# A planner that writes every engine's order: its timing constants, engine occupancy, GpSimd/VectorE exclusion and DMA landings replaced

## The chip, the cores and the metric

The kernel runs on one core of a Trainium2 chip. The metric is device time in microseconds for one launch. The core has five engines with a queue each: TensorE (PE, with its weight loads PEld), VectorE (DVE), ScalarE (ACT), GpSimd (POOL) and SyncE (SP, which here only issues DMAs). Each queue runs its instructions in the order in which the program wrote them, and waits on semaphores for the others.

## The reference

One transformer block on 2048 tokens of width 448: a LayerNorm, then multi-head attention and a mixture of experts side by side, both added to the input.

```python
B, S, D, H = 1, 2048, 448, 16          # F = 1792, E = K = 8
xn = _layernorm(x, axis=-1)
def _A_ref(x, wqkv, wo):
    q, k, v = ...                      # x @ wqkv, 16 heads of 28
    scores = jnp.einsum("bhqd,bhkd->bhqk", q, k) * (Dh ** -0.5)
    p = _softmax(scores, axis=-1)
    o = jnp.einsum("bhqk,bhkd->bhqd", p, v)
    return o.transpose(0, 2, 1, 3).reshape(B, S, D) @ wo
def _B_ref(x, w_gate, w1, w2):         # K = E: every expert gets every token
    gates = _softmax(topk_val, axis=-1)
    for e in range(E):
        h = _silu(xf @ w1[e]) @ w2[e]
        out = out + w * h
return x + _A_ref(xn, wqkv, wo) + _B_ref(xn, w_gate, w1, w2)
```

## The kernel before

All products run in float16 with each operand split into a high and a low half, so one float32 product is three float16 products. The halves are made on the chip: ScalarE rounds the high half, GpSimd or VectorE subtracts to get the low one.

The kernel does not issue instructions directly. `phase0`, `moe` and `attention` register *jobs* with a `Plan`: an engine, a duration `ns`, a function that issues the instructions, a due time `v` in microseconds, and the buffers it reads and writes, from which the dependences follow. `Plan.run` then simulates the chip while the program is being built, and the moment at which a job starts in this simulation is the moment at which its instructions are written to the engine's queue. So the order on each engine is that of the simulated clock, and it is fixed before the launch. The simulation works as follows.

- Whenever an engine is free, `pick` takes the ready job with the least due time whose buffers can be had. Jobs that give a PSUM bank back are moved ahead by `FED`, `HUNGRY` or `S_FED`.
- Before the change an engine is busy for `ns`, and the dependents of the job may start `LAG` of its engine later (PE 180, ACT and DVE 60, POOL 90). A TensorE job's TensorE dependents start without the lag.
- A DMA is a job of SP (a few at the start are ScalarE's) with a `size` in ns. All DMAs share one modelled pipe: `dma = max(dma, t + 1000) + size`, and the data has landed `LAND` = 2000 ns after that.

The MoE's due times run evenly from `M_AT` = 60 to `END` = 2585, attention's from `A_AT` = 0 to `END` less `LEAD` = 130, so the two streams are interleaved over the whole run.

Names and lines that the profile shows:

- Start (`phase0`): `mav` (L333) is the largest weight of the V part, from which `scales` makes a power of two: TensorE at L371 and L374 spreads the maximum, VectorE at L351 to L368 makes the exponent. `flip` turns the first tokens (L703, L706, L710), `split_a` scales the weights `WA` on ScalarE (L567), and `values` (L776) and `queries_keys` (L753) multiply. L312 is the helper behind every plain DMA.
- MoE: the 8 experts' hidden units are cut into 24 groups of 5 or 4 times 128 (`GROUPS`). For each group `load_group` fetches `r1` and `r2`, `group_scales` finds the maxima (L333), and the scale goes through DRAM: a DMA writes 1 KB to `mxs`, a second one reads it back to all partitions as `scmg`, and VectorE job `powers` (L358 to L368) makes the exponents; `both` (L437, L438) follows. `split_w1` and `split_w2` (ScalarE L463, L464, L481, L482; GpSimd L468, L485) make the halves. For each 512 tokens and 128 hidden units `hidden` runs ten full matmuls (L898) into a bank; the rest of four units runs in one job of half-height matmuls (`tails`, L906). `silu` then goes ScalarE tanh (L940), VectorE (L943), ScalarE high half `hh` (L946), GpSimd low half `hl` (L947). `summed` multiplies with `w2` (L962), and VectorE adds to `acc` (L974).
- Attention: 16 heads times 16 tiles of 128 queries. `score` (L1058) fills the one pair of banks tagged "s"; VectorE takes the row extremum (L1062), ScalarE the exponential (L1076), after which the pair is free for the next score. `halves` makes `ph` (ScalarE L1084) and `pl` (VectorE L1087), each in one buffer, and `turn` transposes both by DMA (L1101) into `th` and `tl`. For each four tiles `weigh` runs VectorE `behind` (L1124, L1125), ScalarE `apart` (L1128, L1129), TensorE `lows_of_p` on a quarter of the columns at a time (L1135), ScalarE `lt` (L1150), a DMA transpose to `tt` (L1152), TensorE `highs_of_p` (L1142), VectorE `level` (L1160), GpSimd `lows` and `sums` (L1166 to L1172), VectorE `shares` (L1178, L1179), ScalarE L1184 and GpSimd L1187. After four heads `project` transposes (L1218), multiplies with `wo` (L1228) and adds to `acc` (L1235); `load_wo` splits `wo` (L1207, L1210).

PSUM has eight banks: 0 and 1 are the pair "s", the other six go to everything else.

Of the kernel before, what the change touches and what calls it, by code (L numbers as in the profile page):

```python
# [13 lines left out]
ALU = mybir.AluOpType  # L14
# [40 lines left out]
class Job:  # L55
    __slots__ = ("eng", "ns", "lag", "fn", "v", "seq", "wait", "then", "bufs", "size", "many", "frees")


class Plan:
# [3 lines left out]

    LAG = {"PE": 180, "ACT": 60, "DVE": 60, "POOL": 90, "SP": 0}

# [8 lines left out]

    def add(self, eng, ns, fn, v, r=(), w=(), size=0, after=()):
        j = Job()
        j.eng, j.ns, j.fn, j.v, j.seq, j.size = eng, ns, fn, v, len(self.jobs), size
        j.lag, j.then = self.LAG[eng], []
# [24 lines left out]
        return j  # L103

    def run(self, pools, banks):


        ready = {e: [] for e in self.LAG}
        free = dict.fromkeys(self.LAG, 0)
        live, given = {}, {}  # L110
# [36 lines left out]

        def met(jobs):
            for k in jobs:
                k.wait -= 1  # L150
                if not k.wait:
                    ready[k.eng].append(k)

        while left:
            moved = True
            while moved:
                moved = False
                for e in ready:
# [32 lines left out]
            while events and events[0][0] <= t:  # L191
                _, _, done, j = heapq.heappop(events)
                if not done:
                    if j.eng == "PE":
                        met([k for k in j.then if k.eng == "PE"])
                    continue
                for b in j.bufs:
# [67 lines left out]
def block_kernel(ctx, tc, x, wqkv, wo, w_gate, w1, w2, out):  # L265
# [44 lines left out]
    def dma(out_, in_, v, r=(), w=(), kb=0, eng="SP"):  # L310
        q = {"SP": nc.sync, "ACT": nc.scalar}[eng]
        return add(eng, 600, lambda: q.dma_start(out_(), in_()), v, r, w, size=max(3 * kb, 1))  # L312

# [21 lines left out]
    def scales(name, pool, mx, kinds, v, group=None):  # L335
# [75 lines left out]
    def group_scales(gi, v):  # L411
# [5 lines left out]
        for a in range(2):  # L417
            add(
                "DVE", 150 + 1070 * 256 * g // 1000,
                lambda a=a: abs_max(m4()[:, 0, a : a + 1], r1()[:, 2 * a : 2 * a + 2, 0 : g * P], AX.XY),  # L420
                v, r=[(r1, j, *k) for j in range(g) for k in R1K], w=[(m4, a)],
            )
        for a, (j0, j1) in enumerate(((0, h), (h, g))):
            add(
                "DVE", 150 + 1070 * 448 * (j1 - j0) // 1000,
                lambda a=a, j0=j0, j1=j1: abs_max(m4()[:, 1, a : a + 1], r2()[:, j0:j1, :], AX.XY),
# [12 lines left out]

        add("DVE", 465, both, v, r=[so], w=[th])  # L440
        SC[gi] = so, th

    def gates(gi, v):
        if gi not in GW:
            GW[gi] = b = buf("mp", [P, NT], F32, f"gwe{gi}", tag="gwe", bufs=2)
            th = SC[gi][1]
            add(
                "DVE", 590,
                lambda: nc.vector.tensor_scalar(b(), gw[:, :, GROUPS[gi][0]], th()[:, 1:2], None, op0=ALU.mult),
                v, r=["gw", th], w=[b],  # L450
            )
        return GW[gi]

    def split_w1(gi, j, v):
# [15 lines left out]
        keys = [(r1, j, *k) for k in R1K]  # L470
        add("ACT", 1350, high, v, r=[so], w=[*keys, (w, 0)])
        add("POOL", 1450, low, v, r=[*keys, (w, 0)], w=[(w, 1)])
        W1[gi, j] = w

    def split_w2(gi, j, v):
# [10 lines left out]

        add("ACT", 1260, high, v, r=[so], w=[(r2, j), (w, 0)])
        add("POOL", 1140, low, v, r=[(r2, j), (w, 0)], w=[(w, 1)])
        W2[gi, j] = w
# [16 lines left out]
    def phase0():  # L506
# [159 lines left out]
        def flip_by_dma(c, xn):  # L666

            for j in range(TPC):
# [207 lines left out]
    def moe(at):  # L876
# [8 lines left out]
        def hidden(gi, b, j):  # L885
# [34 lines left out]
            if len(four) == 4:  # L920
# [3 lines left out]
                last[:] = [add(  # L924
                    "PE", 440 + 200, lambda: tails(units), at(spent[0] - 2 * NTERM * Z_NS),
                    r=list(dict.fromkeys(keys)), w=[u[4] for u in units],
                )]
# [7 lines left out]
        def silu(gi, b, j, z, v):  # L935
# [3 lines left out]
            hl = buf("mp", [P, C], F16, f"hl{gi}_{j}_{b}", tag="hl", bufs=RH)  # L939
            add("ACT", 690, lambda: nc.scalar.activation(t(), z(), AF.Tanh, scale=th_()[:, 0:1]), v, r=[z, th_], w=[t])  # L940
            add(
                "DVE", 685,
                lambda: nc.vector.scalar_tensor_tensor(t(), t(), 1.0, z(), op0=ALU.add, op1=ALU.mult),  # L943
                v, r=[z], w=[t],
            )
            add("ACT", 635, lambda: nc.scalar.activation(hh(), t(), AF.Copy), v, r=[t], w=[hh])  # L946
            add("POOL", 1425, lambda: nc.gpsimd.tensor_tensor(hl(), t(), hh(), ALU.subtract), v, r=[t, hh], w=[hl])  # L947
            HS[gi, b, j] = hh, hl
# [58 lines left out]
    def attention(at):  # L1007
# [39 lines left out]
        def score(i, j, v):  # L1047
# [18 lines left out]

            add("DVE", 1330, top, v, r=["cexp"], w=[b, (m, n, j)])

        def expo(i, j, v):
# [7 lines left out]

            add("ACT", 1205, powers, v, r=[s, (m, n, j)], w=[(p, j)])

        def halves(i, v):  # L1080
            p = PR.pop(i)
            PF[i] = h, l = [buf("ap", [P, S], F16, f"p{a}{i}", tag=f"p{a}", bufs=RP) for a in "hl"]
            pk = [(p, 0), (p, 1)]
            add("ACT", 1910, lambda: nc.scalar.activation(h(), p(), AF.Copy, scale=P_SCALE), v, r=pk, w=[h])  # L1084
            add(
                "DVE", 2395,
                lambda: nc.vector.scalar_tensor_tensor(l(), p(), P_SCALE, h(), op0=ALU.mult, op1=ALU.subtract), v,  # L1087
                r=[*pk, h], w=[l],
            )

        def turn(i, v):
# [7 lines left out]
            for b, p, out in ((th, h, lambda: th()), ((tl, q), l, lambda: tl()[:, q])):  # L1099
                add(  # L1100
                    "SP", 2000, lambda out=out, p=p: nc.sync.dma_start_transpose(out(), p()), v, r=[p], w=[b], size=2600  # L1101
                )
# [5 lines left out]
        def weigh(i, v):  # L1108
# [31 lines left out]
            def highs_of_p(n):  # L1140
# [5 lines left out]

            add("DVE", 525, behind, v, r=[(m, n, j) for n in range(NB) for j in range(2)], w=[c, top])
            add("ACT", 580, apart, v, w=[c])
            add("PE", 1070, lows_of_p, v, r=[*((tl, q) for q in range(NB)), vb], w=[zl])
            add("ACT", 595, lambda: nc.scalar.activation(lt(), zl(), AF.Copy, scale=1 / SEL), v, r=[zl], w=[lt])  # L1150
            add(
                "SP", 700, lambda: nc.sync.dma_start_transpose(tt(), lt()), v, r=[lt], w=[tt], size=650,  # L1152
            )
            for n in range(NB):
                add("PE", 424, lambda n=n: highs_of_p(n), v, r=[*ths[n:], vb], w=[av])
            u = buf("ap", [P, NB, 2, n2], F32, f"u{i}", tag="u")
# [31 lines left out]

            add("DVE", 625, level, v, r=[av, c], w=[u])
# [83 lines left out]

M_AT, A_AT, LEAD, END, LAND = 60.0, 0.0, 130.0, 2585.0, 2000
HUNGRY, FED, S_FED = 400.0, 80.0, 130.0
# [23 lines left out]
```

## Time and profile before

| | |
|---|---|
| median of 3 runs | 2629.18 us (2626.14 to 2631.74) |
| the profiled execution | 2628.33 us |
| its span, first to last instruction | 2626.2 us |
| TensorE busy | 2603.8 us, 99% |
| VectorE, ScalarE, GpSimd busy | 82%, 73%, 45% |
| TensorE's first matmul, last y matmuls | from 12.15 us, to about 2622 us |
| DMA engines' mean busy share (hardware queue) | 66.9% |

In the rows of the profile a group of instructions is given as line, engine, operation, tiles (output<-inputs), shape and count; then busy time, mean duration, and the engine's idle time before these instructions with what ended it. In the timeline a row starts with start and length in us, and the brackets hold the idle time of the engine before it. In the list of waits the numbers are the total, the count and the longest. "q" after an engine's name is its queue of DMA issues. In a table by stage each engine has its busy time and count; the last three columns are clock, DMA share and GB/s. Rows of one line or tile give minimum/median/maximum duration in ns and the first and last start. The record of a matmul has a modelled end, so one that is followed at once overlaps the next.

### The profile page before, as it was taken

To read this page: it belongs to the slowest core of one execution; us is meant where nothing else is said; L and a number is where in the kernel's file an instruction comes from. 1 tells how busy PE (TensorE), PEld (TensorE's weight loads), DVE (VectorE), ACT (ScalarE), POOL (GpSimd) and SP (SyncE) were. 2 spreads that over 40 slices of the span, in tenths; PEclk is the share of its full clock that TensorE was granted. 3 is DMA by queue.
4 is the path that set the end of the run, shared out by engine and by line. 5 is a ranking of instruction groups with operands and counts; after the bars stand their busy time and mean duration, and the time that the engine had idled before them with its cause. 6 is when DMAs were issued, how large, how long until landed. Compare 5 with 4: busy or idle time off the path is not lost.

```text
span 2626.2 us, 45450 instructions
## 1 busy us (share of the span) xinstructions
PE 2603.8 (99%) x17149; PEld 1262.4 (48%) x17149; DVE 2157.1 (82%) x3067; ACT 1926.5 (73%) x2482; POOL 1185.1 (45%) x1103
## 2 busy tenths in 40 slices
PE   7999999999999999999999999999999999999999
PEld 3444444444444444444444444444444444444444
DVE  8578888888888888888888888978898779878875
ACT  5586887777877777777777778777777677776762
POOL 2243464436444444534534455454455334543533
PEclk9999999999999999999999999999999999999999
DMA  8657767667676777577675776666676667756663
GB/s 246 177 121 144 168 136 157 137 141 169 136 141 136 148 157 167 123 147 167 131 157 121 164 161 143 149 139 149 148 170 124 142 137 160 162 118 141 141 118 111
DMA packets 1207019, 387.52 MB, mean 148 GB/s; under 512 B 1142928, under 2 KB 1188368, under 8 KB 1206800
## 3 DMA queue, kind: packets, MB, share of 16 engines
q1 hardware_dynamic: 1206240, 384.61, 66.9%
q8 instruction: 134, 2.20, 0.4%
q14 instruction: 85, 0.70, 0.1%
q10 hardware_dynamic: 560, 0.02, 0.0%
HBM read 85.11 MB, written 15.23 MB: 38 GB/s over the span
## 4 chain that ended last, share of the span: by engine, by line
PE 94%; DVE 2%; DMA 1%; POOL 1%; ACT 1%; issue 1%; SPq 0%; DVEq 0%; POOLq 0%; ACTq 0%
PE banks L962 37%; PE banks L898 35%; PE banks L1058 8%; PE banks L1142 4%; PE banks L753 2%; PE banks L1135 2%; PE banks L906 2%; PE banks L776 1%; PE banks L1228 1%; DVE banks L1062 1%; DVE pl L1087 1%; DMA scmg<-mxs 0%; POOL hl L947 0%; ACT pf L1076 0%; ACT ph L1084 0%
## 5 line engine op out<-in xcount | busy, mean ns | idle before, releaser
L898 PE MATMUL banks<-xs,w 128*128 128x512 f16 x4480 | 1035.6, 379 | 1.0 <-DVE acc L974 0.9
L947 POOL TENSOR_TENSOR hl<-t,hh 128x512 f16<-128x512 f32 x448 | 607.9, 1369 | 850.3 <-ACT hh L946 772.2
L962 PE MATMUL banks<-w,hh 128*128 128x448 f16 x3584 | 970.8, 352 | 0.5 <-DVE t L943 0.5
L1076 ACT ACTIVATE pf<-banks,mx 128x1024 f32<-128x1024 f32 x512 | 569.3, 1112 | 368.8 <-DVE mx L1062 340.7
L1062 DVE CUSTOM_DVE_ANT_0 banks<-banks,zero,cneg 128x1024 f32<-128x1024 f32 x512 | 659.6, 1288 | 170.5 <-PE banks L1058 142.1
L898 PEld LDWEIGHTS <-w 128*128 128x128 f16 x4480 | 426.8, 97 | 547.1 <-issue 48.2
L962 PE MATMUL banks<-w,hl 128*128 128x448 f16 x1792 | 631.3, 352 | 0.0
L1087 DVE SCALAR_TENSOR_TENSOR pl<-pf,ph 128x2048 f16<-128x2048 f32 x256 | 611.1, 2387 | 3.9 <-DMA tl<-pl 1.8
L962 PEld LDWEIGHTS <-hh 128*128 128x128 f16 x3584 | 346.7, 98 | 350.9 <-issue 13.4
L1084 ACT ACTIVATE ph<-pf 128x2048 f16<-128x2048 f32 x256 | 487.8, 1905 | 32.2 <-DVE pl L1087 18.1
L940 ACT ACTIVATE t<-banks,the 128x512 f32<-128x512 f32 x448 | 295.9, 683 | 103.4 <-PE banks L898 35.1
L943 DVE SCALAR_TENSOR_TENSOR t<-t,banks 128x512 f32<-128x512 f32 x448 | 296.0, 681 | 63.6 <-ACT t L940 63.0
L974 DVE SCALAR_TENSOR_TENSOR acc<-banks,gwe,acc 128x448 f32<-128x448 f32 x384 | 257.1, 679 | 104.8 <-PE banks L962 103.0
L1058 PE MATMUL banks<-K,Q 112*128 112x512 f16 x1024 | 305.8, 379 | 2.3 <-ACT pf L1076 2.2
L946 ACT ACTIVATE hh<-t 128x512 f16<-128x512 f32 x448 | 267.5, 623 | 47.0 <-PE banks L962 35.5
L962 PEld LDWEIGHTS <-hl 128*128 128x128 f16 x1792 | 174.7, 98 | 164.3
L468 POOL TENSOR_TENSOR w<-r,w 128x512 f16<-128x512 f32 x112 | 156.0, 1400 | 140.4 <-ACT w L464 130.9
L485 POOL TENSOR_TENSOR w<-r,w 128x448 f16<-128x448 f32 x112 | 132.1, 1185 | 106.4 <-ACT w L482 103.2
L1058 PEld LDWEIGHTS <-Q 112*128 112x128 f16 x1024 | 95.2, 98 | 108.5 <-issue 17.0
L333 DVE TENSOR_REDUCE mx<-r 128x1 f32<-128x1280 f32 (+3 forms) x96 | 124.9, 1310 | 1.4 <-DMA r<-in_B_w_dram 1.4
L1142 PEld LDWEIGHTS <-th 128*128 128x128 f16 x4096 | 118.2, 96 | 13.7 <-issue 0.4
L1142 PE MATMUL banks<-V,th 128*128 128x57 f16 x4096 | 119.7, 188 | 0.0
(141 smaller groups left out, 1512.7 us busy)
## 6 DMA issues: line engine op xcount, KB each, us to landing
r<-in_B_w_dram SPq DMA_DIRECT2D x16, 1120.0 KB
r<-in_B_w_dram SPq DMA_DIRECT2D x16, 960.0 KB
K<-qk SPq DMA_DIRECT2D x128, 56.0 KB
Q<-qk SPq DMA_DIRECT2D x256, 28.0 KB
r<-in_B_w_dram SPq DMA_DIRECT2D x8, 896.0 KB
r<-in_B_w_dram SPq DMA_DIRECT2D x8, 768.0 KB
r<-in_B_w_dram SPq DMA_DIRECT2D x32, 160.0 KB
vs<-vt SPq DMA_DIRECT2D x4, 1024.0 KB
```

What stands on the lines that cost most here:

```text
L898: nc.tensor.matmul(z(), rows(w)[:, blk, :], xx, start=(i == 0 and not late), stop=(i == NTERM - 2 and late))
L940: add("ACT", 690, lambda: nc.scalar.activation(t(), z(), AF.Tanh, scale=th_()[:, 0:1]), v, r=[z, th_], w=[t])
L943: lambda: nc.vector.scalar_tensor_tensor(t(), t(), 1.0, z(), op0=ALU.add, op1=ALU.mult),
L946: add("ACT", 635, lambda: nc.scalar.activation(hh(), t(), AF.Copy), v, r=[t], w=[hh])
L947: add("POOL", 1425, lambda: nc.gpsimd.tensor_tensor(hl(), t(), hh(), ALU.subtract), v, r=[t, hh], w=[hl])
L962: nc.tensor.matmul(y()[:, 0:D], a, wv, start=(i == 0 and u == 0), stop=(i == g - 1 and u == 2))
L1058: nc.tensor.matmul(b()[:, cs], q()[:, q0 : q0 + P], k()[:, cs], start=True, stop=True)
L1062: nc.vector.tensor_tensor_reduce(b(), b(), zero.to_broadcast([P, 2 * C]), cneg, HUGE, op0=ALU.add, op1=ALU.min, accum_out=m()[:, n, j : j ...
L1076: nc.scalar.activation(p()[:, 2 * j * C : 2 * (j + 1) * C], s(), AF.Exp, bias=m()[:, n, j : j + 1], scale=-1.0)
L1084: add("ACT", 1910, lambda: nc.scalar.activation(h(), p(), AF.Copy, scale=P_SCALE), v, r=pk, w=[h])
L1087: lambda: nc.vector.scalar_tensor_tensor(l(), p(), P_SCALE, h(), op0=ALU.mult, op1=ALU.subtract), v,
L1142: nc.tensor.matmul(a()[:, n, kt // (NKT // 2), 0:n2], ths[n]()[:, kt], vb()[:, kt, 0:n2], start=(n == 0 and kt == 0), stop=(n == NB - 1 an ...
```

## The change

Every job still issues the same instructions. The planner's clock changes:

- An engine is free again after `ns` less `LEAVE`; a job's result is there after `ns` plus `more` (a default per engine in `MORE`), and reaches the dependent after `REACH` of the engine that receives it. Buffers come free some 50 ns after the result.
- VectorE jobs with `port` > 0 and GpSimd jobs exclude each other: the one that comes second waits, or the GpSimd job's end is moved (`later`); `steps` is the number of instructions in a GpSimd job, at whose bounds VectorE may get in.
- DMAs: issue 400 ns for 600, `LAND` 2500 for 2000, 900 less for transposes; transposes have smaller sizes (1650 for 2600, 450 for 650), and the two DMAs of a group's scale larger ones (`kb` 350 for 1, 400 for 128).
- Nearly all `ns` get new values.

The diff, cut to its core:

```diff
-    LAG = {"PE": 180, "ACT": 60, "DVE": 60, "POOL": 90, "SP": 0}
+    LEAVE = {"PE": 0, "ACT": 105, "DVE": 82, "POOL": 40, "SP": 0}
+    MORE = {"PE": 227, "ACT": 0, "DVE": 0, "POOL": 0, "SP": 0}
+    REACH = {"PE": 52, "ACT": 34, "DVE": 32, "POOL": 76, "SP": 60}
+    LEAD_IN, RACE = 143, 188
...
-        def met(jobs):
+        def met(jobs, same=False):
             for k in jobs:
                 k.wait -= 1
-                if not k.wait:
+                k.at = max(k.at, t if same else t + self.REACH[k.eng])
+                if k.wait:
+                    continue
+                if k.at > t:
+                    heapq.heappush(events, (k.at, k.seq, 2, k))
+                else:
                     ready[k.eng].append(k)
+
+        def later(ns):
+
+            pool[1] += ns
+            free["POOL"] += ns
+            pool[3].due += ns
+            heapq.heappush(events, (free["POOL"], pool[3].seq, 3, pool[3]))
...
-                    free[e] = t + j.ns
-                    end = t + j.ns + j.lag
+                    wait = 0
+                    if j.port:
+                        want, step = t + j.port, pool[2]
+                        if pool[1] > want:
+                            if pool[0] + self.RACE < want:
+                                k = -(-(want - pool[0]) // step)
+                                wait = min(pool[0] + k * step, pool[1]) - want
+                                if pool[1] - want - wait > self.LEAD_IN:
+                                    later(j.ns - j.port - self.LEAD_IN)
+                            else:
+                                later(t + j.ns - max(want, pool[0] + self.LEAD_IN))
+                        taken = t + j.ns + wait
+                    if e == "POOL":
+                        wait = max(0, taken - t - self.LEAD_IN)
+                        pool[:] = [t + wait, t + j.ns + wait, j.ns // j.steps, j]
+                    free[e] = t + j.ns - self.LEAVE[e] + wait
+                    end = t + j.res + wait
                     if j.size:
                         dma = max(dma, t + 1000) + j.size
-                        end = dma + (LAND if j.v > 1 else 1000)
+                        end = dma + (LAND if j.v > 1 else 1000) - (900 if j.ns > 1000 else 0)
+                    j.due = end
...
-        return add(eng, 600, lambda: q.dma_start(out_(), in_()), v, r, w, size=max(3 * kb, 1))
+        return add(eng, 400, lambda: q.dma_start(out_(), in_()), v, r, w, size=max(3 * kb, 1))
...
-            dma(lambda: mxs[group], lambda: mx(), v, r=[mx], w=[("mxs", group)], kb=1)
+            dma(lambda: mxs[group], lambda: mx(), v, r=[mx], w=[("mxs", group)], kb=350)
...
-                r=[("mxs", group)], w=[pb], kb=128,
-            )
-        add("DVE", 600 + 300 * n + (0 if pe else 420), powers, v, r=[pb], w=[bm, ea, si, so])
+                r=[("mxs", group)], w=[pb], kb=400,
+            )
+        add("DVE", 600 + 300 * n if pe else 1397, powers, v, r=[pb], w=[bm, ea, si, so], port=0 if pe else 500)
...
-            add("ACT", 690, lambda: nc.scalar.activation(t(), z(), AF.Tanh, scale=th_()[:, 0:1]), v, r=[z, th_], w=[t])
+            add("ACT", 686, lambda: nc.scalar.activation(t(), z(), AF.Tanh, scale=th_()[:, 0:1]), v, r=[z, th_], w=[t])
...
-            add("POOL", 1425, lambda: nc.gpsimd.tensor_tensor(hl(), t(), hh(), ALU.subtract), v, r=[t, hh], w=[hl])
+            add("POOL", 1159, lambda: nc.gpsimd.tensor_tensor(hl(), t(), hh(), ALU.subtract), v, r=[t, hh], w=[hl])
...
-            add("PE", 2 * Z_NS, product, v, ..., w=[b])
+            add("PE", 2 * Z_NS, product, v, ..., w=[b], more=280)
-            add("DVE", 1330, top, v, r=["cexp"], w=[b, (m, n, j)])
+            add("DVE", 1292, top, v, r=["cexp"], w=[b, (m, n, j)], more=58)
-            add("ACT", 1205, powers, v, r=[s, (m, n, j)], w=[(p, j)])
+            add("ACT", 1114, powers, v, r=[s, (m, n, j)], w=[(p, j)])
...
-                "DVE", 2395,
+                "DVE", 2283,
...
-                r=[*pk, h], w=[l],
+                r=[*pk, h], w=[l], port=138,
...
-                    "SP", 2000, lambda out=out, p=p: nc.sync.dma_start_transpose(out(), p()), v, r=[p], w=[b], size=2600
+                    "SP", 1600, lambda out=out, p=p: nc.sync.dma_start_transpose(out(), p()), v, r=[p], w=[b], size=1650
...
-            add("DVE", 525, behind, v, r=[(m, n, j) for n in range(NB) for j in range(2)], w=[c, top])
+            add("DVE", 358, behind, v, r=[(m, n, j) for n in range(NB) for j in range(2)], w=[c, top], port=300)
...
-            add("POOL", 1180, lows, v, r=[tt, c], w=[ls])
-            add("POOL", 1570, sums, v, r=[ls], w=[u])
-            add("DVE", 690, shares, v, r=[u], w=[rl, os_])
+            add("POOL", 1286, lows, v, r=[tt, c], w=[ls], steps=2)
+            add("POOL", 1818, sums, v, r=[ls], w=[u], steps=3)
+            add("DVE", 560, shares, v, r=[u], w=[rl, os_], port=360)
...
-M_AT, A_AT, LEAD, END, LAND = 60.0, 0.0, 130.0, 2585.0, 2000
+M_AT, A_AT, LEAD, END, LAND = 60.0, 0.0, 130.0, 2585.0, 2500
```

More of the change, by code (lines that the diff above doesn't have):

```diff
@@ L55 @@
 class Job:
-    __slots__ = ("eng", "ns", "lag", "fn", "v", "seq", "wait", "then", "bufs", "size", "many", "frees")
+    __slots__ = ("eng", "ns", "fn", "v", "seq", "wait", "then", "bufs", "size", "many", "frees", "res", "port", "steps", "at", "due")
 class Plan:
-    LAG = {"PE": 180, "ACT": 60, "DVE": 60, "POOL": 90, "SP": 0}
+    LEAVE = {"PE": 0, "ACT": 105, "DVE": 82, "POOL": 40, "SP": 0}
+    MORE = {"PE": 227, "ACT": 0, "DVE": 0, "POOL": 0, "SP": 0}
+    REACH = {"PE": 52, "ACT": 34, "DVE": 32, "POOL": 76, "SP": 60}
+    LEAD_IN, RACE = 143, 188
     def __init__(self):
@@ L73, in buf, with add @@
         return b
-    def add(self, eng, ns, fn, v, r=(), w=(), size=0, after=()):
+    def add(self, eng, ns, fn, v, r=(), w=(), size=0, after=(), more=None, port=0, steps=1):
         j = Job()
         j.eng, j.ns, j.fn, j.v, j.seq, j.size = eng, ns, fn, v, len(self.jobs), size
-        j.lag, j.then = self.LAG[eng], []
+        j.res, j.then = ns + (self.MORE[eng] if more is None else more), []
+        j.port, j.steps, j.at, j.due = port, steps, 0, 0
         deps = set(after)
@@ L105, in run @@
     def run(self, pools, banks):
-        ready = {e: [] for e in self.LAG}
-        free = dict.fromkeys(self.LAG, 0)
+        ready = {e: [] for e in self.LEAVE}
+        free = dict.fromkeys(self.LEAVE, 0)
+        pool = [0, 0, 0, None]
+        taken = 0
         live, given = {}, {}
@@ L192, in run @@
                 _, _, done, j = heapq.heappop(events)
+                if done == 2:
+                    ready[j.eng].append(j)
+                    continue
+                if done == 3:
+                    continue
                 if not done:
                     if j.eng == "PE":
-                        met([k for k in j.then if k.eng == "PE"])
+                        met([k for k in j.then if k.eng == "PE"], True)
+                    continue
+                if done == 1:
+                    if j.due > t:
+                        heapq.heappush(events, (j.due, j.seq, 1, j))
+                        continue
+                    met([k for k in j.then if not (j.eng == k.eng == "PE")])
+                    heapq.heappush(events, (t + self.REACH["PE"] - 2, j.seq, 4, j))
                     continue
@@ L438, in both @@
             nc.vector.tensor_tensor(th()[:, 1:2], th()[:, 0:1], col(so, 3), ALU.mult)
-        add("DVE", 465, both, v, r=[so], w=[th])
+        add("DVE", 340, both, v, r=[so], w=[th], port=300)
         SC[gi] = so, th
@@ L470, in split_w1 @@
         keys = [(r1, j, *k) for k in R1K]
-        add("ACT", 1350, high, v, r=[so], w=[*keys, (w, 0)])
-        add("POOL", 1450, low, v, r=[*keys, (w, 0)], w=[(w, 1)])
+        add("ACT", 1372, high, v, r=[so], w=[*keys, (w, 0)])
+        add("POOL", 1160, low, v, r=[*keys, (w, 0)], w=[(w, 1)])
         W1[gi, j] = w
@@ L485, in low @@
             nc.gpsimd.tensor_tensor(w()[:, 1, :], r2()[:, j, :], w()[:, 0, :], ALU.subtract)
-        add("ACT", 1260, high, v, r=[so], w=[(r2, j), (w, 0)])
-        add("POOL", 1140, low, v, r=[(r2, j), (w, 0)], w=[(w, 1)])
+        add("ACT", 1265, high, v, r=[so], w=[(r2, j), (w, 0)])
+        add("POOL", 1038, low, v, r=[(r2, j), (w, 0)], w=[(w, 1)])
         W2[gi, j] = w
@@ L687, in flip_by_dma @@
                 add("ACT", 560, high, v(), r=[(xn[j], 0)], w=[(b, 0)])
-                add("DVE", 800, low, v(), r=[(xn[j], 0), (b, 0)], w=[(b, 1)])
+                add("DVE", 686, low, v(), r=[(xn[j], 0), (b, 0)], w=[(b, 1)], port=138)
                 add("POOL", 760, again, v(), r=[(b, 0)], w=[(b, 2)])
@@ L924, in hidden @@
                 last[:] = [add(
-                    "PE", 440 + 200, lambda: tails(units), at(spent[0] - 2 * NTERM * Z_NS),
-                    r=list(dict.fromkeys(keys)), w=[u[4] for u in units],
+                    "PE", 620, lambda: tails(units), at(spent[0] - 2 * NTERM * Z_NS),
+                    r=list(dict.fromkeys(keys)), w=[u[4] for u in units], more=-75,
                 )]
@@ L1145, in highs_of_p @@
                     )
-            add("DVE", 525, behind, v, r=[(m, n, j) for n in range(NB) for j in range(2)], w=[c, top])
-            add("ACT", 580, apart, v, w=[c])
-            add("PE", 1070, lows_of_p, v, r=[*((tl, q) for q in range(NB)), vb], w=[zl])
-            add("ACT", 595, lambda: nc.scalar.activation(lt(), zl(), AF.Copy, scale=1 / SEL), v, r=[zl], w=[lt])
+            add("DVE", 358, behind, v, r=[(m, n, j) for n in range(NB) for j in range(2)], w=[c, top], port=300)
+            add("ACT", 442, apart, v, w=[c])
+            add("PE", 1052, lows_of_p, v, r=[*((tl, q) for q in range(NB)), vb], w=[zl], more=155)
+            add("ACT", 597, lambda: nc.scalar.activation(lt(), zl(), AF.Copy, scale=1 / SEL), v, r=[zl], w=[lt])
             add(
-                "SP", 700, lambda: nc.sync.dma_start_transpose(tt(), lt()), v, r=[lt], w=[tt], size=650,
+                "SP", 1200, lambda: nc.sync.dma_start_transpose(tt(), lt()), v, r=[lt], w=[tt], size=450,
             )
             for n in range(NB):
-                add("PE", 424, lambda n=n: highs_of_p(n), v, r=[*ths[n:], vb], w=[av])
+                add("PE", 424, lambda n=n: highs_of_p(n), v, r=[*ths[n:], vb], w=[av], more=170)
             u = buf("ap", [P, NB, 2, n2], F32, f"u{i}", tag="u")
```

25 lines of the change are left out of this document (12 added, 13 removed).

## The prediction

> **What bounds the kernel now.** I read the page's parts 1 and 2 first, then PE's waits, then stages, then single stalls in the timeline.
>
> ```profile
> span 2626.2 us, 45450 instructions
> PE 2603.8 (99%) x17149; PEld 1262.4 (48%) x17149; DVE 2157.1 (82%) x3067; ACT 1926.5 (73%) x2482; POOL 1185.1 (45%) x1103
> PEclk9999999999999999999999999999999999999999
> ```
>
> TensorE is busy 2603.8 of 2626.2 us at an undiminished clock; only 22.4 us of its time are idle. Its waits, and two stages:
>
> ```profile
> PE banks L371 <- DVE mav L333: 12.2, 1, 12.2
> PE banks L1058 <- ACT pf L1076: 2.2, 3, 1.2
> PE banks L776 <- ACT WA L567: 2.0, 1, 2.0
> PE banks L898 <- DVE acc L974: 0.9, 1, 0.9
> PE banks L962 <- DVE t L943: 0.5, 2, 0.3
> PE banks L906 <- DVE acc L1235: 0.2, 1, 0.2
> PE banks L374 <- DVE scdv L352: 0.2, 1, 0.2
> ...
> 300.00:500.00 200.00, 200.00 (x1327) 96.97 (x1326) 171.06 (x236) 156.16 (x200) 100.51 (x90) 1.00 0.69 145
> 2000.00:2400.00 400.00, 398.16 (x2707) 193.45 (x2706) 329.50 (x448) 300.92 (x379) 184.25 (x166) 1.00 0.67 143
> ```
>
> Of the idle time 12.2 us lie before the first matmul, 2.2 more at the start (L776, L374), about 4 after the last matmul, and only 2.2 + 0.9 + 0.5 + 0.2 = 3.8 us in the 2500 us between. A little more is hidden, since a record is longer than its slot:
>
> ```profile
> 1003.78 4.48 PE L898 MATMUL banks<-xs,w 128*128 128x512 f16 x20
> L898 PE MATMUL banks<-xs,w 128*128 128x512 f16 x4480 | 1035.6, 379 | 1.0 <-DVE acc L974 0.9
> ```
>
> Twenty matmuls take 4.48 us, so (4.48 - 0.38)/19 = 0.216 us each, though one record is 379 ns: a wait up to 0.16 us does not show, and each of the 7 steady waits hides that much. Steady stalls are then 3.8 + 7 x 0.16, about 5 us. This caps what any order of the same instructions can win in the steady part: 5 of 2628 us, 0.19%.
>
> **The change part by part.** Only numbers and rules inside the planner change; every job issues the same instructions. 17149 matmuls stay, so do all DMAs with their real sizes (the new kb of `mxs` and `pb` enters only the planner's clock). What can change is the order on each queue, hence the waits. Against the trace the new numbers stand so:
>
> ```profile
> L940 ACT ACTIVATE t<-banks,the x448: 667/686/705, 127.4 to 2601.9; 128x512 f32<-128x512 f32 x150
> 2597.26 1.27 ACT L940 ACTIVATE t<-banks,the 128x512 f32<-128x512 f32 x2 [5.94 <-PE banks L906]
> L947 POOL TENSOR_TENSOR hl<-t,hh x448: 1148/1159/3309, 129.6 to 2612.0; 128x512 f16<-128x512 f32 x150
> ```
>
> One tanh lasts 686 ns, but two together 1.27 us, so the second starts 0.58 us after the first: that is the new ns (686) less LEAVE (105). The old plan booked 690 ns of occupancy. For `hl` the new 1159 is the median; the 3309 is a GpSimd instruction that waited, which the old flat 1425 + 90 left out. So the new clock is nearer the chip for the engines. I take each part:
>
> *Exclusion and late broadcasts (the gain).* These are the two stalls on L1058 over 0.6 us, one on L898 and one on L962:
>
> ```profile
> 2282.89 0.55 SPq L312 DMA_DIRECT2D mxs<-mxr  x1
> 2288.39 0.33 SPq L312 DMA_DIRECT2D scmg<-mxs  x1
> 2291.66 0.42 DVE L358 TENSOR_REDUCE scbg<-scmg 128x2 f32<-128x256 f32 x1 [2.06 <-DMA scmg<-mxs]
> 2292.11 1.15 DVE L361 TENSOR_SCALAR scbg<-scbg 128x2 f32<-128x2 f32 x1
> 2292.08 1.16 POOL L947 TENSOR_TENSOR hl<-t,hh 128x512 f16<-128x512 f32 x1
> 2296.54 0.59 PE L1058 MATMUL banks<-K,Q 112*128 112x512 f16 x2 [1.20 <-ACT pf L1076]
> ...
> 2033.05 1.21 DVE L1179 TENSOR_TENSOR os<-u,rl 128x112 f32<-128x112 f32 x1 [0.29 <-POOL u L1172]
> 2036.72 0.59 PE L1058 MATMUL banks<-K,Q 112*128 112x512 f16 x2 [0.64 <-ACT pf L1076]
> ...
> 1379.59 1.17 DVE L368 TENSOR_SCALAR scog<-scig 128x4 int32<-128x4 int32 x1
> 1381.40 0.81 PE L898 MATMUL banks<-xs,w 128*128 128x512 f16 x3 [0.90 <-DVE acc L974]
> ...
> 617.47 3.04 DVE L1125 TENSOR_TENSOR c<-top,mx 128x8 f32<-128x8 f32 x1
> 618.22 2.27 POOL L947 TENSOR_TENSOR hl<-t,hh 128x512 f16<-128x512 f32 x2
> ```
>
> At 2282.89 the write of `mxs` is issued; its reader goes out 5.50 us later where the old plan reckons 1000 + 3 + 2000 ns, and VectorE, which runs in order, stands 2.06 us for the broadcast. Then a tiny TENSOR_SCALAR takes 1.15 us because GpSimd started `hl` 0.03 us before. The score's reduction queued behind, the exponential behind that, and TensorE 1.20 us. The others are the same kind: small VectorE instructions of 1.2 and 3 us beside GpSimd. The new plan reckons 1000 + 1050 + 2500 = 4.55 us and 1000 + 1200 + 2500 = 4.70 us for the two DMAs, together 9.25 against 2291.66 - 2282.89 = 8.77 here, and holds such VectorE jobs while GpSimd runs. Gain: (1.20 + 0.16) + (0.64 + 0.16) + (0.90 + 0.16) + (0.3 + 0.16) = 3.7 us at most, none at least; I take 3.5, since both causes are modelled with the right size. What is late next is whatever job now stands in these places, and TensorE has other banks to work on.
>
> The Trainium skill (SBUF — State Buffer, "SBUF: two separate sides") says that the pair of ports which VectorE and GpSimd share is a lock held for the whole instruction, and the loser blocks. The 2033.05 row agrees with that. The 617.47 row does not fully: three microseconds reach over two GpSimd instructions, so VectorE did not get in between them. By the rule this last stall of 0.46 us goes too; by the row, about 0.5 us stays, and the sum by one or the other is 3.7 or 3.2.
>
> *DMA landings of the transposes (the loss).* Old plan: 1000 + 2600 + 2000 = 5.6 us from issue to use; new: 1000 + 1650 + 2500 - 900 = 4.25 us. TensorE uses them as soon as the plan allows:
>
> ```profile
> 1440.32 2.47 SPq L1101 DMA_TRANSPOSE tl<-pl  x1
> 1445.96 1.05 PE L1135 MATMUL banks<-tl,V 128*32 128x512 f16 x16
> ...
> 448.45 2.35 SPq L1101 DMA_TRANSPOSE tl<-pl  x1
> 452.96 2.29 DVE L1087 SCALAR_TENSOR_TENSOR pl<-pf,ph 128x2048 f16<-128x2048 f32 x1 [0.99 <-DMA tl<-pl]
> ...
> L1101 SPq DMA_TRANSPOSE th<-ph x256: 1317/1624/5776, 142.6 to 2575.3; - x128
> 2271.48 4.19 SPq L1101 DMA_TRANSPOSE th<-ph  x1
> 2279.25 1.91 ACT L1084 ACTIVATE ph<-pf 128x2048 f16<-128x2048 f32 x1 [1.00 <-DMA th<-ph]
> ```
>
> Issue to use is 5.64 us here, the tightest of the 64 groups. Landing took at most 452.96 - 448.45 = 4.5 us in one place and 7.8 us in another, beside other transfers. So 1.35 us less cover can uncover waits at 128 places (64 `lows_of_p`, 64 first `highs_of_p`), queued behind which is all of TensorE. Bounds: zero, if the landings that count are quick; 128 x (4.5 - 4.25) = 32 us, if each waits a quarter microsecond. No TensorE wait names a transpose today, in all 128, so I take the low side: 1 in 10 waiting 0.1 us or so, 1.3 us.
>
> *Occupancy and latency of ACT, VectorE, GpSimd, PE.* Shorter occupancy lets the plan fill ACT and VectorE more tightly; chains keep their length. For one score to the next through the bank pair: old 432 + 180 + 1390 + 1265 = 3267 ns, new 432 + 280 + 32 + 1350 + 34 + 1114 + 50 = 3292. That is 25 ns more cover 512 times. Gain or loss: 0, bounds -1 to +3 us (512 x 6 ns).
>
> *SP.* Issue costs go from 600 to 400 and 2000 to 1600; L1101 has a median of 1.62. SP is not behind a TensorE wait now: 0.
>
> *Order at the start.* ACT served four flips before WA (2.0 us at L776). A different order there is worth -2 to +2; I take 0. The 12.2 us wait for DMA and `mav` stays.
>
> *Mode changes.* Around each packed block TensorE loses some time: the row below starts 0.28 us after the last L962 at 2588.82, not 0.19. There are 112 + 64 such blocks in any order; only neighbours can save 0.09 each: 0, within 1.
>
> ```profile
> 2588.82 0.35 PE L962 MATMUL banks<-w,hl 128*128 128x448 f16 x1
> 2589.10 1.05 PE L1135 MATMUL banks<-tl,V 128*32 128x512 f16 x16
> 2606.35 15.90 PE banks L962 x84
> ```
>
> *The end.* After the last projection 84 matmuls (15.90 us) of MoE follow; they cover attention's chain as long as attention ends no more than that later: 0.
>
> Sum: -3.5 + 1.3 + 0 = -2.2 us on the profiled execution's 2628.33 us (span 2626.2 and 2.1 around it), so 2626.1. The median of the runs is 0.85 above that execution: 2627.0.
>
> **The rivals.**
> A: *The transposes' cover was needed* (slower). Place: L1135 and the first L1142 of a group. For: 7.8 us landings exist, and the plan's 4.25 is below them. Against: no such wait today. It decides as soon as the waits pass 3.5 + 5.3 = 8.8 us, that is 0.07 us at each of 128 places. At 0.1 us: 2629.2 - 3.5 + 12.8 = 2638.5.
> B: *All steady stalls go and the start tightens*: 2629.2 - 5 - 2 = 2622.2. For: the causes seen are the ones modelled. Against: it needs every one.
> C: *The stalls move.* A wait removed here returns at another bank or buffer, as when VectorE cannot enter between two GpSimd instructions: 2629.2, give or take 1.5.
> D: *Balance shifts.* If attention falls more than 15.9 us behind MoE, its last chain stands bare and TensorE idles: some 30 us more lag gives 2629.2 + 14 = 2643. Nothing speaks for it but that the exclusion holds VectorE, 82% busy, longer.
>
> **How the numbers follow.** About 0.2% (5.3 us) is what a measurement of this kernel tells from no change. Forecast 0.40 (2624 to 2629), C 0.22, B 0.15, A 0.17, D 0.06. Faster: B and a little of the forecast, 0.19; slower: A and D less A's mild end, 0.20; the rest 0.61. Range 2621.5 (B) to 2637 (A at 0.09 us a place), with less than 2 in 10 outside.
>
> **What would show it.** Right: TensorE's steady waits fall from 3.8 to below 2 us; L358 no longer waits for `scmg`; durations of L361, L1125 and L1179 come closer to their usual ones; matmul counts and times are unchanged. A shows as TensorE waiting for `DMA tl<-pl` or `DMA th<-ph`, D as idle slices after 2590 us. A change of more than 5 us downwards can only come from the start, and would make me wrong.

## The result, and the profile after

The changed kernel is slower: 2661.43 us median (2659.57 to 2662.93) against 2630.46 us for the kernel before, a ratio of 1.0118 (95% interval 1.0103 to 1.0133), 31 us. Forecast were 2627.0 us and a range that ended at 2637.

The page's first lines, and TensorE's waits in the changed kernel (lines are 45 higher than before: L1180 is `lows_of_p`, L1187 `highs_of_p`, L1103 the score, L1121 the exponential, L821 `values`):

```profile
span 2660.8 us, 45559 instructions
PE 2611.5 (98%) x17149; PEld 1266.2 (48%) x17149; DVE 2155.7 (81%) x3067; ACT 1919.0 (72%) x2482; POOL 1192.0 (45%) x1103
```
```profile
PE banks L416 <- DVE mav L378: 12.3, 1, 12.3
PE banks L1180 <- DMA tl<-pl: 11.0, 11, 3.3
PE banks L1103 <- ACT pf L1121: 4.8, 7, 1.8
PE banks L1187 <- DMA th<-ph: 4.7, 2, 2.7
PE banks L1180 <- issue: 3.6, 2, 2.9
PE banks L821 <- ACT WA L612: 2.0, 1, 2.0
PE banks L798 <- DVE ql L807: 1.2, 2, 1.1
PE banks L1273 <- DMA ohl<-ost: 1.0, 1, 1.0
PE banks L1007 <- DVE t L988: 1.0, 1, 1.0
PE banks L1007 <- DVE acc L1019: 1.0, 2, 0.6
PE banks L1103 <- DMA K<-qk: 0.9, 1, 0.9
```

The matmuls are the same 17149, the first one waits the same 12 us, `values` the same 2.0 us. The difference lies in the steady part: its waits were 3.8 us and are now 11.0 + 4.8 + 4.7 + 3.6 + 1.2 + 1.0 + 1.0 + 1.0 + 0.9 and two of 0.3, about 30 us. Idle time rose from 22.4 to 2660.8 - 2611.5 = 49.3 us, 27 of the 34.6 us between the spans. The other 7.7 us are in a longer busy time. Three stretches of half clock, shown at the end, make up to 5 us of it; the rest, perhaps waits too short to leave a gap, was not traced.

Over half of the new waiting names the transposes (11.0 + 4.7 us). One of these waits, the DMA issues of SP first, then TensorE:

```profile
583.11 4.29 SPq L1146 DMA_TRANSPOSE th<-ph  x1
587.58 0.45 SPq L357 DMA_DIRECT2D scmg<-mxs  x1
588.12 4.47 SPq L1146 DMA_TRANSPOSE tl<-pl  x1
...
594.88 1.34 PE L1180 MATMUL banks<-tl,V 128*32 128x512 f16 x16 [3.26 <-DMA tl<-pl]
```

The last `tl` of the group is issued at 588.12, right behind a scale's broadcast, and TensorE gets it at 594.88, 6.8 us later, where the new plan reckons 4.6 us (4.25 and some time for the broadcast). This makes two thirds of the wait. The other third comes from before the issue: the `th` ahead of it held SP for 4.29 us, for which the plan books 1.6, and `tl` followed 5.01 us behind it instead of the planned 3.86. So the 5.6 us from issue to use of the old plan would have covered about 1 of the 3.26 us. Such long issues are not new: of the 512 transposes of `th` and `tl`, 58 held SP for over 2.5 us before and 52 after.

What the planner learned to expect did not go away on the chip. Mean durations of the instructions that VectorE and GpSimd keep each other from, first before, then after:

```profile
L1125 DVE TENSOR_TENSOR c<-top,mx 128x8 f32<-128x8 f32 x64 | 25.0, 391 | 2.2
L1087 DVE SCALAR_TENSOR_TENSOR pl<-pf,ph 128x2048 f16<-128x2048 f32 x256 | 611.1, 2387 | 3.9 <-DMA tl<-pl 1.8 <-ACT ph L1084 1.6
L947 POOL TENSOR_TENSOR hl<-t,hh 128x512 f16<-128x512 f32 x448 | 607.9, 1369 | 850.3 <-ACT hh L946 772.2 <-DVE t L943 22.6 <-PE banks L898 14.1
```
```profile
L1170 DVE TENSOR_TENSOR c<-top,mx 128x8 f32<-128x8 f32 x64 | 23.1, 361 | 2.2
L1132 DVE SCALAR_TENSOR_TENSOR pl<-pf,ph 128x2048 f16<-128x2048 f32 x256 | 610.7, 2385 | 47.4 <-ACT ph L1129 33.3 <-DMA tl<-pl 13.4 <-ACT pf L1121 0.3
L992 POOL TENSOR_TENSOR hl<-t,hh 128x512 f16<-128x512 f32 x448 | 618.2, 1393 | 809.5 <-ACT hh L991 737.3 <-PE banks L1103 20.0 <-PE banks L1187 14.1
```

391 and 361 ns, 2387 and 2385, 1369 and 1393: the mutual waits are much the same in amount. New is the idle time before `pl`, 47.4 us for 3.9: VectorE, which in the old order nearly always had something to do there, now stands and waits for ScalarE and for the transposes to give the buffer back. The order has become just-in-time. This idle time is no measure of the loss, though: one of the experiments (f3) loses more and has only 17.0 us of it.

### The profile page after: what moved, and what is told of

The parts are those of the page before. It is cut to its first block, busy times and chain, and to the rows that moved or that the text cites. A ratio compares the mean times of both kernels' runs of the same rounds, so it can differ in the third digit from the quotient of the medians.

```text
span 2660.8 us, 45559 instructions
## 1 busy us (share of the span) xinstructions
PE 2611.5 (98%) x17149; PEld 1266.2 (48%) x17149; DVE 2155.7 (81%) x3067; ACT 1919.0 (72%) x2482; POOL 1192.0 (45%) x1103
## 4 chain that ended last, share of the span: by engine, by line
PE 82%; DVE 6%; DMA 5%; ACT 4%; issue 2%; POOL 1%; SPq 0%; DVEq 0%; ACTq 0%; POOLq 0%
PE banks L1007 33%; PE banks L943 30%; PE banks L1103 7%; DMA tl<-pl 3%; PE banks L1187 3%; PE banks L1180 2%; DVE pl L1132 2%; PE banks L951 2%; PE banks L798 2%; DVE banks L1107 2%; PE banks L821 1%; ACT pf L1121 1%; PE banks L1273 1%; ACT ph L1129 1%; DVE t L988 1%
## 5 line engine op out<-in xcount | busy, mean ns | idle before, releaser
L992 POOL TENSOR_TENSOR hl<-t,hh 128x512 f16<-128x512 f32 x448 | 618.2, 1393 | 809.5 <-ACT hh L991 737.3
L1121 ACT ACTIVATE pf<-banks,mx 128x1024 f32<-128x1024 f32 x512 | 569.0, 1111 | 400.6 <-DVE mx L1107 383.7
L1132 DVE SCALAR_TENSOR_TENSOR pl<-pf,ph 128x2048 f16<-128x2048 f32 x256 | 610.7, 2385 | 47.4 <-ACT ph L1129 33.3
L991 ACT ACTIVATE hh<-t 128x512 f16<-128x512 f32 x448 | 269.7, 625 | 69.1 <-PE banks L1007 49.3
L1103 PE MATMUL banks<-K,Q 112*128 112x512 f16 x1024 | 306.1, 380 | 6.3 <-ACT pf L1121 4.8
L530 POOL TENSOR_TENSOR w<-r,w 128x448 f16<-128x448 f32 x112 | 138.0, 1244 | 95.5 <-ACT w L527 88.2
L1103 PEld LDWEIGHTS <-Q 112*128 112x128 f16 x1024 | 96.8, 98 | 115.7 <-issue 19.7
L1211 POOL TENSOR_TENSOR ls<-tt 128x232 f32<-128x232 f16 x64 | 40.3, 629 | 240.9 <-DMA tt<-lt 231.5
L1187 PEld LDWEIGHTS <-th 128*128 128x128 f16 x4096 | 119.1, 96 | 23.9 <-issue 5.9
L1187 PE MATMUL banks<-V,th 128*128 128x57 f16 x4096 | 122.1, 188 | 4.9 <-DMA th<-ph 4.7
```

Source lines behind the costliest of these rows:

```text
L991: add("ACT", 621, lambda: nc.scalar.activation(hh(), t(), AF.Copy), v, r=[t], w=[hh])
L992: add("POOL", 1159, lambda: nc.gpsimd.tensor_tensor(hl(), t(), hh(), ALU.subtract), v, r=[t, hh], w=[hl])
L1103: nc.tensor.matmul(b()[:, cs], q()[:, q0 : q0 + P], k()[:, cs], start=True, stop=True)
L1121: nc.scalar.activation(p()[:, 2 * j * C : 2 * (j + 1) * C], s(), AF.Exp, bias=m()[:, n, j : j + 1], scale=-1.0)
L1187: nc.tensor.matmul(a()[:, n, kt // (NKT // 2), 0:n2], ths[n]()[:, kt], vb()[:, kt, 0:n2], start=(n == 0 and kt == 0), stop=(n == NB - 1 an ...
```

## The experiments

Each run is compared with runs of the kernel before on the same chip (medians there 2632 to 2635 us), so ratios are what to compare.

My first theory, T1, was rival A of the prediction: the transposes' thinner cover is the loss. T2 said that the engines' tighter occupancies are, T0 that any new order is worth as much.

**e1_after_late_turns** and **e2_before_early_turns**: the transposes' landing alone, undone in the new plan and done in the old.

```diff
# e1, on the changed planner
-end = dma + (LAND if j.v > 1 else 1000) - (900 if j.ns > 1000 else 0)
+end = dma + (LAND if j.v > 1 else 1000) - (900 if j.ns > 1000 else 0) + (1350 if j.ns == 1600 else 0)
# e2, on the planner before
-end = dma + (LAND if j.v > 1 else 1000)
+end = dma + (LAND if j.v > 1 else 1000) - (1350 if j.ns == 2000 else 0)
```

> The changed planner, with the landing of the th and tl transposes modelled 1.35 us later again (5.6 us from issue, as before the change). Theory T1 (the thinner cover of the transposes is the loss; L1180 and L1187 wait 21 us more in the changed kernel): about 2640 us, and TensorE's waits for tl and th gone. Theory T2 (the tighter engine occupancies cost the time, the transposes only show where it surfaces): 2657 to 2664 us, the waits turning up under other names. Theory T0 (any new order is worth some 15 us up or down): anything from 2625 to 2665.

> The old planner, with only the landing of the th and tl transposes modelled 1.35 us earlier (4.25 us from issue, as in the change). T1: 2645 to 2655 us, with TensorE waiting some 20 us for tl and th. T2: 2626 to 2634 us. T0: anything from 2625 to 2660.

**e3_after_land_10ns** and **e4_before_land_10ns**: `LAND` 2510 for 2500, and 2010 for 2000.

> The changed planner with LAND 2510 for 2500, a number without meaning that shakes the order. T1 and T2: within 5 us of the changed kernel, 2656 to 2666 us. T0: 2640 to 2680 us, showing that the loss is partly the luck of one order.

> The old planner with LAND 2010 for 2000, which shakes its order as little. T1 and T2: within 5 us of the kernel before, 2625 to 2635 us. T0: 2615 to 2650 us.

Measured: e1 1.0081 (1.0063 to 1.0099), e2 1.0009 (1.0000 to 1.0018), e3 1.0118 (1.0103 to 1.0133), e4 0.9990 (0.9980 to 1.0000). T0 falls as far as two shakes can show it: they give the time of the unshaken orders within 0.1%, although in e3's plan 1588 of TensorE's 2796 jobs stand at another place of its queue than in the changed kernel's. T1 falls as the main cause: late landings win back 0.4 of the 1.2%, and early ones cost the old plan only 0.1%, no more than e4's shake gives. By its ratio e1 lies between the times of T1 and of T2, nearer to T2's. In e1 the waits did in part turn up under another name:

```profile
PE banks L1103 <- ACT pf L1121: 11.5, 18, 1.5
...
PE banks L1180 <- DMA tl<-pl: 6.9, 4, 4.5
...
PE banks L1187 <- DMA th<-ph: 2.1, 1, 2.1
```

(The profiled execution of e1 is the slowest of its four, 2663 us, so the kinds of waits count here, not their sum.)

The next four undo one part of the change, or do one part alone. T3: the old plan's too long occupancies were spare time that absorbed what no planner models. T4: the exclusion rule is wrong. T5: the DMA model is too short.

**f1_after_no_leave**: `LEAVE = {"PE": 0, "ACT": 0, "DVE": 0, "POOL": 0, "SP": 0}` in the changed planner.

> The changed planner with LEAVE set to 0 for all engines: an engine stays booked for the whole latency of a job, 105 ns (ACT), 82 ns (VectorE) and 40 ns (GpSimd) longer than the chip holds it. Theory T3 (the old plan's spare occupancy absorbed what no planner models; the true occupancy leaves no spare): 1.000 to 1.005 times the kernel before, 2630 to 2645 us. Theory T4 (the exclusion rule lets VectorE in where the chip does not): unchanged, about 1.012, 2660 us. Theory T5 (the DMA model is too short): 1.010 to 1.013.

**f2_after_no_port**: every `port` 0 in the changed planner.

```diff
-        j.port, j.steps, j.at, j.due = port, steps, 0, 0
+        j.port, j.steps, j.at, j.due = 0, steps, 0, 0
```

> The changed planner without the exclusion of GpSimd and VectorE (every port 0). T3: no better than the changed kernel, 1.010 to 1.018, since the true waits are now not in the plan at all. T4: clearly better, 1.000 to 1.006. T5: 1.010 to 1.015.

**f3_before_leave**: the old planner with the new `LEAVE`, nothing else.

```diff
-                    free[e] = t + j.ns
+                    free[e] = t + j.ns - self.LEAVE[e]
```

> The old planner with the LEAVE of the change alone: engines come free 105, 82 and 40 ns earlier, results, lags and DMAs as before. T3: 1.004 to 1.012, the loss or a good part of it appears. T4 and T5: 0.998 to 1.002.

**f4_after_old_dma**: the changed planner with all DMA numbers of before (600 and 2000 ns, sizes 2600 and 650, `LAND` 2000 without the 900 off, `kb` 1 and 128).

> The changed planner with every DMA number as before the change (issue 600 and 2000 ns, sizes 2600 and 650, LAND 2000 without the 900 off, the scales' DMAs 1 and 128 KB). T5: 1.000 to 1.004. T3 and T4: 1.007 to 1.012, a little better than the changed kernel as with the late transposes alone (1.008).

Measured: f1 1.0024 (1.0015 to 1.0033), f2 1.0281 (1.0259 to 1.0304), f3 1.0137 (1.0121 to 1.0153), f4 1.0047 (1.0032 to 1.0062). T3 has the direction right from both sides: without `LEAVE` four fifths of the loss are gone, and `LEAVE` alone costs the old planner as much as the whole change does (the two intervals overlap). Its sizes were off: f2 and f3 lie above its intervals and f4 below. T4 falls: without the exclusion the tight plan loses another 1.6%. T5 has a part: the DMA numbers are worth 0.7%, a little less than it said. The parts do not add; either spare alone, of the engines or of the DMAs, takes away most of the loss. In f1 TensorE's waits for `tl` fell from 11.0 to 0.4 us, and these two fell from 4.7 and 4.8 us:

```profile
PE banks L1187 <- DMA th<-ph: 3.7, 3, 2.9
...
PE banks L1103 <- ACT pf L1121: 1.5, 3, 0.9
```

TensorE's waits in f3, where nothing but the occupancy changed (lines are 2 higher than before):

```profile
PE banks L1060 <- ACT pf L1078: 21.4, 27, 4.2
PE banks L373 <- DVE mav L335: 11.9, 1, 11.9
PE banks L964 <- DVE acc L976: 3.1, 4, 1.6
PE banks L755 <- DVE ql L764: 3.1, 4, 1.6
```

The score waited 3 times for the exponential before, 2.2 us; here 27 times, 21.4 us. Its matmuls now stand in TensorE's queue at the moment that the plan thinks right, VectorE and ScalarE are late, and everything behind the score in TensorE's queue waits too. What makes them late is of two kinds. The first row below is a `pl` of 3.24 us, where 2.29 is usual, beside GpSimd; the score at 311.23 waits 1.75 us behind it. The other rows are the longest wait: the issue of one `th` holds SP for 9.35 us, ScalarE stands 5.87 us until that transpose gives `ph` back, and TensorE 4.21 us.

```profile
305.53 3.24 DVE L1089 SCALAR_TENSOR_TENSOR pl<-pf,ph 128x2048 f16<-128x2048 f32 x1
...
946.55 9.35 SPq L1103 DMA_TRANSPOSE th<-ph  x1
959.63 1.91 ACT L1086 ACTIVATE ph<-pf 128x2048 f16<-128x2048 f32 x1 [5.87 <-DMA th<-ph]
962.59 1.01 PE L1060 MATMUL banks<-K,Q 112*128 112x512 f16 x2 [4.21 <-ACT pf L1078]
```

How much of the loss belongs to each kind was not separated.

Four more put the parts together and look for the prediction's gain.

**g1_after_no_leave_old_dma**: f1 and f4 together.

> The changed planner with LEAVE 0 and all DMA numbers as before the change; what is left of the change is the exclusion, the latencies from the trace and the receiving engine's latency. T3 (spare in the planner's clock, of engines and of DMAs, is what keeps TensorE fed): 0.996 to 0.999 times the kernel before, since both spares are back and the exclusion removes its stalls of about 3 us. Rival T6 (the latencies and hops of the change lose time of their own): 1.001 to 1.004.

**g2_after_no_leave_late_turns**: f1 and e1 together.

> The changed planner with LEAVE 0 and only the th and tl transposes landing 1.35 us later. T3: 0.997 to 1.000, the 4.5 us that TensorE waits for th and the 2.4 us for tl with LEAVE 0 alone are gone. T6: 1.001 to 1.004.

**g3_before_scale_dma**: the old planner with `kb` 350 and 400 for the scales' DMAs.

> The old planner with only the two DMAs of a group's scale modelled at 350 and 400 KB. The prediction's gain term for the late broadcast (1.4 us, one stall): 0.999 to 1.000, and VectorE's 6.9 us of waits for the broadcast gone. If planner numbers that are nearer the trace cost time by themselves: 1.001 or more.

**g4_before_leave_dve**: f3 with VectorE's 82 ns alone.

> The old planner with the LEAVE of VectorE alone (82 ns). T3 with VectorE as the engine that runs late (82% busy, held by GpSimd): 1.005 to 1.012, most of the 1.0137 that all three gave. If ScalarE's spare is what counts: 0.999 to 1.003.

Measured: g1 0.9982 (0.9973 to 0.9991), g2 1.0002 (0.9993 to 1.0011), g3 0.9994 (0.9985 to 1.0003), g4 1.0033 (1.0021 to 1.0044). g1 comes out below the kernel before: 2627.55 against 2631.69 us. With both spares back, the rest of the change (the exclusion and the latencies from the trace) loses nothing, so T6 falls; whether it is the cause of the 0.18% is not shown. e4's shake, a number without meaning, gave 0.10%, and no shake of g1 was tried. TensorE's waits in g1 are no shorter than before; after the start they are 2.2 + 0.7 + 0.6 + 0.3 = 3.8 us again, and 2.0 us at L798:

```profile
PE banks L416 <- POOL xn L706: 11.2, 1, 11.2
PE banks L1103 <- ACT pf L1121: 2.2, 4, 0.8
PE banks L821 <- ACT WA L612: 2.0, 1, 2.0
PE banks L798 <- DVE the L482: 2.0, 1, 2.0
PE banks L1103 <- DMA K<-qk: 0.7, 1, 0.7
PE banks L1180 <- DMA tl<-pl: 0.6, 1, 0.6
```

g2 lies between T3's and T6's intervals, and one wait of 3.9 us for `tl` is left in it. (Its expectation gives f1 waits of 4.5 and 2.4 us; the trace of f1 has 3.7 and 0.4.) g3 cannot be told from no change, and 2.9 of VectorE's 6.9 us of waits for the broadcast stayed. g4 fell between the intervals of both its theories: VectorE's occupancy alone costs 0.33%, not the larger part.

The last three ask whose spare it is, whether the loss is gradual, and whether more spare helps.

**h1_before_leave_act**: f3 with ScalarE's 105 ns alone.

> The old planner with the LEAVE of ScalarE alone (105 ns). T3 with the spare of both engines counting: 1.004 to 1.011, so that this and the 1.0033 of VectorE alone make up the 1.0137 of all three. If VectorE's spare is the only one that counts and the rest was GpSimd's: 0.999 to 1.003.

**h2_after_half_leave**: `LEAVE` 52, 41 and 20 in the changed planner.

> The changed planner with half the LEAVE (52, 41 and 20 ns). T3: between the two ends of 1.0118 and 1.0024, 1.004 to 1.009. If one threshold decides (a chain that just fits or does not): at one of the two ends.

**h3_more_spare_old_dma**: f4 with `LEAVE` of minus 60 for ScalarE, VectorE and GpSimd.

> The changed planner with the old DMA numbers and LEAVE of minus 60 ns for ScalarE, VectorE and GpSimd: each engine booked 60 ns longer than the job's latency. T3: 0.996 to 0.999, no slower than with LEAVE 0 (0.9982), perhaps 1 to 3 us faster. If the spare of LEAVE 0 was already enough, and more only holds work back: 0.998 to 1.002.

Measured: h1 1.0034 (1.0022 to 1.0046), h2 1.0066 (1.0052 to 1.0080), h3 1.0012 (1.0003 to 1.0021). h1 missed its interval from below: ScalarE alone costs as much as VectorE alone, and both together with GpSimd's 40 ns (1.0137) twice their sum. That would fit a chain in which the spare of one engine catches what another is late; it is not shown, and GpSimd's 40 ns alone were not tried. h2 lies in the middle, as T3 said: at this one point between the ends the loss is gradual. h3 is slower than g1 by 0.3%, against T3's expectation. TensorE's longest wait there after the start, and its last stage by engine, show what too much spare costs:

```profile
PE banks L1273 <- DMA ohl<-ost: 2.5, 2, 1.7
```
```profile
2600.00:2660.00 60.00, 28.41 (x206) 14.21 (x204) 18.67 (x28) 8.51 (x14) 9.06 (x10) 0.93 0.26 66
```

The projections (L1273) have come to the very end, the last matmul at 2630.3 us, and TensorE waits for their transposes: attention ends too late, the mechanism of rival D. Whether other due times (`LEAD`) would win this back was not tried.

The planner computes an end on its own clock while the program is built. It is no measurement of the chip, but it can be set beside the spans of the profiled executions:

| kernel | planner's end, us | span on the chip, us | chip later by, us |
|---|---|---|---|
| before | 2611.6 | 2626.2 | 14.6 |
| after | 2605.4 | 2660.8 | 55.4 |
| f1, no `LEAVE` | 2606.4 | 2636.6 | 30.2 |
| f2, no exclusion | 2606.5 | 2706.5 | 100.0 |
| f3, before with `LEAVE` | 2608.6 | 2670.8 | 62.2 |
| f4, old DMA numbers | 2605.1 | 2640.0 | 34.9 |
| g1, no `LEAVE`, old DMA | 2608.6 | 2624.7 | 16.1 |
| h3, more spare, old DMA | 2627.4 | 2634.6 | 7.2 |

The change improved the plan by 6 us and made the chip miss it by 41 us more. So the loss does not lie in the plan itself, but in how far the chip falls behind it. In this table much spare (h3) lengthens the plan and shortens the miss, and g1 has the least sum of the eight.

## Why the prediction was wrong

The step that failed is "Occupancy and latency of ACT, VectorE, GpSimd, PE", taken at 0 with bounds of -1 to +3 us. Undoing its `LEAVE` takes 1.0118 to 1.0024, 25 us; doing it alone costs 1.37%, 36 us. I checked there that the numbers are true (they are: 0.58 us from tanh to tanh) and that a lone chain keeps its length, and did not ask what the false ones had been good for. The profile before had a hint in its rows: VectorE instructions of 1.15 and 3.04 us where 0.17 is usual, `hl` between 1148 and 3309 ns, transposes whose issue took up to 5.8 us, and yet TensorE 99% busy. Something covered delays of this size, and the runs show that the 82, 105 and 40 ns per job by which the plan overbooked VectorE, ScalarE and GpSimd were a large part of it. How the cover divides among the kinds of delay was not measured. The prediction asked for the cover of one chain, not for that of the queues.

The second failure is a size: "1 in 10 waiting 0.1 us" for the transposes. The trace after has 11.0 + 3.6 us at L1180 and 4.7 us at L1187, over half of the bounds' width and not their low side; late landings alone give back 0.37%, about 10 us. The term *SP*, put at 0, may have a share too: the stall shown at 594.88 has a third of its length from SP's late issue, and all DMA numbers together give back 0.7%; the issue costs alone were not tried. "No TensorE wait names a transpose today" was true, but said only that 5.6 us sufficed. Rival A had the place and the way of the loss; at 2638.5 us it was too small. A likely reason, not shown by itself, is that it left out the engines' and SP's lateness, which delays the issue of the transposes too.

Not contradicted was the cap on the gain (about 5 us: the best order, g1, won 0.18% or 4.7 us, interval 2.4 to 7.1). Right were the unchanged start (2.0 us at L821 again), the unchanged number of matmuls, and the direction of the exclusion, whose removal costs 1.6% in the tight plan. The gain of 3.5 us itself was not shown: g1 wins about as much, but its steady waits are not shorter, and its scale DMAs are the old ones, so the late broadcast was not the part that paid. The range was wrong in kind: gains were bounded by the 5 us of stalls there are, losses by rival A at 0.09 us a place alone, and the upper end should have been set by the delays that the old plan's spare hid.

By the Trainium skill (SBUF — State Buffer, "SBUF: two separate sides") the loser of the shared ports blocks for the whole instruction of the other. f2 does not test this rule; it shows that leaving the exclusion out of the tight plan costs 1.6%. The row at 617.47 shows that a queue of GpSimd instructions can hold VectorE longer than one of them. Whether the planner would gain from that second fact was not tried.

## What to carry to other kernels

A plan fixed before the launch needs spare time where the chip is irregular, and constants that look wrong, here by some 100 ns a job, may be that spare. Make a planner's model truer only one part at a time, and keep a margin on occupancies and landings on purpose: here the truer exclusion and latencies with the old margins (g1) made the one version that was clear of the kernel before on the fast side, by 0.18%. When the bottleneck engine is 99% busy, price a change of order by what it can uncover, not by the idle time it can remove.

## What the runs showed of the hardware

Short stalls can cost TensorE its clock. Three stretches in the changed kernel ran at half clock (the granted clock, 0.50, is the third column from the right), each about 3.4 us long; the kernel before has none there, from its first 23 us to its last matmul. First the three stretches, then TensorE's rows around two of them:

```profile
288.30:291.70 3.40, 2.73 (x19) 0.96 (x20) 0.73 (x2) 2.98 (x5) 2.29 (x2) 0.50 0.00 0
595.50:598.90 3.40, 3.40 (x17) 0.72 (x9) 3.37 (x5) 1.98 (x3) 2.95 (x1) 0.50 0.55 147
1653.60:1657.04 3.44, 3.39 (x34) 1.58 (x35) 2.29 (x1) 2.05 (x4) 0.25 (x1) 0.50 0.58 133
```
```profile
287.24 0.60 PE L1187 MATMUL banks<-V,th 128*128 128x57 f16 x16 [1.98 <-DMA th<-ph]
288.97 1.90 PE L1180 MATMUL banks<-tl,V 128*32 128x512 f16 x16 [1.13 <-DMA tl<-pl]
1653.65 1.90 PE L1180 MATMUL banks<-tl,V 128*32 128x512 f16 x16 [2.91 <-issue]
```

The `lows_of_p` of a group take 1.90 us in these two rows, where the row of the kernel before has 1.05. The stalls at the stretches were 1.98 and 1.13 us, 3.26 us (at 594.88) and 2.91 us. A stretch of 3.4 us at half clock loses up to 1.7 us, so the three together lose up to 5 us, by estimate.

Not every stall of this size did it: one of 2.74 us, ended at 1337.09, was followed by none. The starts of the three stretches lie 90 and 310 times 3.413 us apart, so time can be cut into windows of 3.413 us on that grid. TensorE's busy time in the windows ahead of the stretches (first, second and last row) and in the two that share the stall of 2.74 us (in such a table of TensorE alone the busy time is the second number):

```profile
284.88:288.29 3.41, 0.98 (x31) 1.00 1.24 147
592.08:595.49 3.41, 0.61 (x12) 1.00 1.00 224
1332.77:1336.18 3.41, 1.58 (x50) 1.00 1.58 162
1336.18:1339.59 3.41, 1.80 (x34) 1.00 0.92 227
1650.21:1653.62 3.41, 0.53 (x20) 1.00 1.06 130
```

Idle in these windows were 2.43, 2.80 and 2.88 us against 1.83 and 1.61. The same count in all seventeen profiles has 20 windows at full clock with more than 2.0 us idle, and each is followed by half clock; no window with less than 1.85 us idle is, and in between it goes either way. So here it is the idle share of one window that decides, somewhat over half of it, and not the length of a stall.

The Trainium skill (TensorE: Matmul & The Clock Gate, "Part 1: The HAM clock gate (the 'warmup' mystery)") says that the array falls to half clock after an idle window of about 3.4 us, with windows of 3413 ns that run freely. The length of the stretches and the grid agree; but none of the windows above was idle as a whole, and the first stretch came with stalls of only 1.98 and 1.13 us.
